# The memory's products behind a tenancy of scores, and the first block's q projected whole before k

## The chip, the cores and the metric

One core of one Trainium2 chip runs the whole kernel. The metric is the device time of one launch in microseconds (us). For every execution the profile also gives its span on the core, some 1.7 us shorter than the time, and the mean granted clock of TensorE, where 1.000 is full speed. Ratios below are the mean time of one kernel's fast runs over that of the other's of the same rounds, so they are not quite the ratio of the medians that stand beside them. All runs here count as fast, those with a mean clock of 0.998 too, and every kernel named below gave correct results.

## The reference, cut to what matters

The kernel is a transformer block over 2048 tokens of width 1024: layer norm, attention of 32 heads in four blocks of 512 tokens with a running memory, a projection, a second layer norm and a gated network of width 3584.

```python
g = sigmoid(beta)
for s in range(4):                       # blocks of 512 tokens
    p = softmax(qs @ ks.T * scale + mask)
    a_dot = p @ vs
    num = phi(qs) @ M                    # what earlier blocks left
    den = phi(qs) @ z + 1e-6
    outs.append(g * (num / den) + (1 - g) * a_dot)
    M = M + phi(ks).T @ vs               # "products for the memory's state"
    z = z + phi(ks).sum(tokens)
h  = x + o @ wo
h2 = h + (silu(ln(h) @ w1) * (ln(h) @ w3)) @ w2
```

## The kernel before

TensorE works in three tilings. Full matmuls use the whole array (128*128 in the views). Scores take four row tiles at once ("tenancies" of the banks that ScalarE's exponentials then empty; the four matmuls of the first start within 0.01 us, at 20.760 to 20.770 in before's trace). The attention's sums take four column tiles (128*32), many small matmuls in one go, and the products for M and z are column tiles too. In the kernel before they are an operation of their own, which the scheduler put into the column stretches:

```python
def memory(self, s, half, gr):
    ...                                  # cut
    def emit(e, gr):
        ...                              # 64 matmuls of 33 columns
        e.matmul(self.ps[32*j:32*j+32, ...], pkn[:, 4*i+kc, 32*j:32*j+32],
                 v[:, kc, g0+i, j, 0:33], start=kc == 0, stop=kc == 3,
                 tile_position=(0, 32*j))
    o = self.g.op("pe", 16 * 42.0, emit, ...)
    o.mode = "col"
    ...                                  # VectorE adds the bank to Macc
```

The first block's tokens come in four tiles x0 to x3. In the head of the kernel q and k are projected for half of their columns, token quarter by token quarter as the tiles get ready, and the other half follows whole:

```python
loads = [x0, x1, wq[:, :, 0:256], x2, x3, wk[:, :, 0:256],
         wq[:, :, 256:512], wk[:, :, 256:512], wv]        # put in words here
work = [(w, i, Group(...)) for w in (wq, wk) for i in range(2)]
for c0 in range(0, 512, 128):
    for w, i, gr in work:                # 8 matmuls of 128 columns
        ...
```

TensorE starts with warm-up matmuls on zeros, `self.warm(12)`, and one more, `self.warm(1, ...)`, between x0's transposes and q's first matmuls.

The softmax here doesn't subtract the row's maximum and nothing guards it: scores larger than these inputs give would overflow.

## Time and profile before

| kernel before | us |
|---|---|
| times of three runs | 895.78, 896.09, 897.34 |
| span of the profiled execution | 895.0 |
| TensorE busy, share of the span | 98% |
| first 128-column matmul of q | 7.70 |
| all 160 matmuls of 128 columns done (128 of projections, 32 transposes) | 18.07 |
| first scores | 20.76 |
| issue hole in the fifth set of products | 1.21 |

TensorE bounds the kernel, so what counts is where it stands or changes tiling. The lines of the views are shown in the prediction. A line of a timeline reads: start in us, busy time, engine, source line, operation, output and inputs by name, tile shape, element shape, count, and in brackets how long the engine was idle before it and what ended that. PE is TensorE and PEld its weight loads, DVE is VectorE, ACT ScalarE, POOL GpSimd and SP SyncE, whose queue issues the transfers (all that the page lists are its).

### The profile page before, as it was taken

Reading aid. Unit: us, or ns where it says so; the run is one execution under the profiler, and the core shown is the slowest. Engines: PE = TensorE matmul, PEld = TensorE weight load, DVE = VectorE, ACT = ScalarE, POOL = GpSimd, SP = SyncE. Lnnn points to the kernel's source line nnn. Section 1 sums busy time; section 2 is a strip of 40 time slices with the busy share of each in tenths; the row PEclk is TensorE's granted clock in tenths of the full one; section 3 lists DMA queues with packets and bytes.
Section 4 is the critical chain, followed back from the end, with each engine's and each line's share of the span. In section 5 each row is a group of like instructions: output and inputs, shape, how many; then the busy total and the mean of one; then the engine's idle time right before and its main releaser. Section 6 shows DMA issues by size and latency. Waiting matters only on the chain.

```text
span 895.0 us, 13604 instructions
## 1 busy us (share of the span) xinstructions
PE 880.6 (98%) x5833; PEld 403.4 (45%) x5921; DVE 417.6 (47%) x631; ACT 287.9 (32%) x306; POOL 173.8 (19%) x226
## 2 busy tenths in 40 slices
PE   8999999999999999999999999999999999999998
PEld 5343444444444444444444444444444444444445
DVE  5784848585848485754555311211334333331111
ACT  6767766656565646111111100000111111110000
POOL 2553445353534343100200000000000000000000
PEclk9999999999999999999999999999999999999999
DMA  7899755634541221753475211113223221301110
GB/s 235 227 212 271 187 142 147 187 92 130 165 99 57 72 70 58 225 153 92 120 224 140 85 36 36 30 46 90 64 60 94 71 71 48 95 24 41 40 37 30
DMA packets 146540, 96.32 MB, mean 108 GB/s; under 512 B 45488, under 2 KB 133680, under 8 KB 146480
## 3 DMA queue, kind: packets, MB, share of 16 engines
q1 hardware_dynamic: 146480, 95.45, 38.8%
q8 instruction: 47, 0.77, 0.4%
q14 instruction: 13, 0.11, 0.0%
HBM read 76.55 MB, written 8.39 MB: 95 GB/s over the span
## 4 chain that ended last, share of the span: by engine, by line
PE 97%; issue 1%; DVE 1%; DMA 1%; ACT 0%; SPq 0%; ACTq 0%; DVEq 0%
PE ps L708 89%; PE ps L1107 4%; PE ps L1057 3%; DMA xs<-in_A_x_dram 1%; PE ps L985 0%; PE ps L1184 0%; ACT et L1069 0%; PE ps L1100 0%; DVE t L1260 0%; DVE hm L1265 0%; PE ps L720 0%; SPq L299 0%; DVE R L1163 0%; ACT sg L1257 0%; DVE Nsb L1171 0%
## 5 line engine op out<-in xcount | busy, mean ns | idle before, releaser
L708 PE MATMUL ps<-hnT,w1b 128*128 128x512 bf16 x876 | 218.4, 379 | 1.4 <-issue 0.3
L708 PE MATMUL ps<-hnT,w3b 128*128 128x512 bf16 x873 | 217.4, 379 | 1.5 <-issue 0.5
L1257 ACT ACTIVATE sg<-ps 128x512 bf16<-128x512 f32 x112 | 66.9, 597 | 403.1 <-PE ps L708 403.1
L708 PE MATMUL ps<-w2b,hm 128*128 128x512 bf16 (+1 forms) x907 | 195.3, 372 | 0.9
L1069 ACT ACTIVATE et<-ps 128x2048 bf16<-128x2048 f32 x80 | 150.0, 1875 | 39.3 <-PE ps L1057 38.9
L1260 DVE SCALAR_TENSOR_TENSOR t<-sg,ps 128x512 bf16<-128x512 bf16 x112 | 76.8, 685 | 169.4 <-ACT sg L1257 169.2
L708 PEld LDWEIGHTS ps<-w2b,hm 128*128 128x128 bf16 x924 | 90.4, 98 | 103.2
L708 PEld LDWEIGHTS ps<-hnT,w1b 128*128 128x128 bf16 x896 | 86.5, 98 | 105.5 <-issue 8.2
L708 PEld LDWEIGHTS ps<-hnT,w3b 128*128 128x128 bf16 x896 | 86.5, 98 | 105.4 <-issue 2.9
L1078 POOL TENSOR_SCALAR_AFFINE_SELECT et<-et 128x512 bf16<-128x512 bf16 x96 | 84.0, 881 | 126.2 <-ACT et L1069 126.0
L1265 DVE SCALAR_TENSOR_TENSOR hm<-t,ps 128x512 bf16<-128x512 bf16 x112 | 76.7, 686 | 50.5 <-PE ps L708 47.9
L1289 DVE TENSOR_TENSOR ob<-hr,ps 128x512 bf16<-128x512 bf16 (+1 forms) x33 | 22.1, 671 | 143.0 <-PE ps L708 143.0
L708 PE MATMUL ps<-wo,oT 128*128 128x512 bf16 x249 | 60.7, 380 | 0.6 <-issue 0.3
L708 PE MATMUL ps<-xnT,wp 128*128 128x512 bf16 (+1 forms) x345 | 59.7, 320 | 1.4 <-issue 0.6
L708 PE MATMUL ps<-hnT,wp 128*128 128x512 bf16 x250 | 59.0, 380 | 0.7 <-issue 0.6
L708 PEld LDWEIGHTS ps<-xnT,wp 128*128 128x128 bf16 x352 | 27.7, 98 | 26.9 <-issue 3.6
L708 PEld LDWEIGHTS ps<-wo,oT 128*128 128x128 bf16 x256 | 23.9, 98 | 29.8 <-issue 2.9
L708 PEld LDWEIGHTS ps<-hnT,wp 128*128 128x128 bf16 x256 | 23.6, 98 | 29.8 <-issue 3.8
L1200 POOL TENSOR_TENSOR oT<-Nsb,R 128x512 bf16<-128x512 f32 x23 | 35.8, 1569 | 4.1 <-DVE R L1197 4.1
L1163 DVE STREAM_TRANSPOSE R<-Rc 128x1024 f32<-128x1024 f32 x28 | 33.6, 1222 | 0.1
L1229 DVE TENSOR_TENSOR h<-h,ps 128x512 bf16<-128x512 bf16 x32 | 21.7, 680 | 25.1 <-PE ps L708 24.9
L1057 PE MATMUL ps<-qT,kT 32*128 32x128 bf16 (+3 forms) x512 | 31.7, 301 | 0.0
(82 smaller groups left out, 520.9 us busy)
## 6 DMA issues: line engine op xcount, KB each, us to landing
w1b<-in_B_w_dram SPq DMA_DIRECT2D x28, 512.0 KB, 3.9
w3b<-in_B_w_dram SPq DMA_DIRECT2D x28, 512.0 KB, 3.8
wp<-in_A_wv_dram SPq DMA_DIRECT2D x8, 1024.0 KB, 5.5
wp<-in_A_wq_dram SPq DMA_DIRECT2D x7, 1024.0 KB, 5.9
wp<-in_A_wk_dram SPq DMA_DIRECT2D x7, 1024.0 KB, 5.7
w2b<-in_B_w_dram SPq DMA_DIRECT2D x7, 1024.0 KB, 8.0
xs<-in_A_x_dram SPq DMA_DIRECT2D x16, 256.0 KB, 5.6
h<-in_A_x_dram SPq DMA_DIRECT2D x16, 256.0 KB, 3.7
```

The source lines that it names most:

```text
L708: return [e.matmul(p[0](gr), p[1], p[2], start=p[3], stop=p[4]) for p in part]
L1057: ins.append(e.matmul(self.bank(gr, j, 512 - 128 * kc, off), k[r, g0 + g, 128 * kc:128 * kc + 128], q[r, g0 + g, 128 * kc:512], start=True ...
L1069: return [e.activation(et[:, :, :], src, AF.Exp, scale=self.scale)]
L1078: self.pool_op(lambda e, v=v, pat=pat: e.affine_select(v, v, pattern=pat, compare_op=ALU.is_ge, fill=0.0, base=0, channel_multiplier=-1), ...
L1107: ins.append(e.matmul(self.ps[32 * i:32 * i + 32, b * 512 + 128 * kc:(b + 1) * 512], lhsT(i, kc, j), at[i, kc][:, j, :], start=kc == 0 and ...
L1163: return self.dve_op(lambda e: e.transpose(out, src), dve_ns(1024), [Rc[:, t, 2 * n:2 * n + 2, :]], [dst], 2)
L1200: self.either(lambda e, out=out, Ns=Ns, R1=R1: e.tensor_tensor(out, Ns, R1, op=ALU.add), 512, 2, [Ns, R1], [out], 2)
L1229: self.g.op("dve", dve_ns(512), lambda e, gr, hs=hs: [e.tensor_tensor(hs, hs, self.bank(gr), op=ALU.add)], reads=[hs], writes=[hs], cls=1, ...
L1257: self.g.op("act", act_ns(512), lambda e, gr, sg=sg: [e.activation(sg, self.bank(gr), AF.Tanh, scale=0.5)], writes=[sg], cls=0, group=gg)
L1260: e.scalar_tensor_tensor(t1, sg, 1.0, self.bank(gr), op0=ALU.add, op1=ALU.mult)], reads=[sg], writes=[t1], cls=0,
L1265: e.scalar_tensor_tensor(dst, t1, 0.5, self.bank(gr), op0=ALU.mult, op1=ALU.mult)], reads=[t1], writes=[dst], cls=0,
L1289: self.g.op("dve", dve_ns(n), lambda e, gr, hs=hs, ob=ob, n=n: [e.tensor_tensor(ob, hs, self.bank(gr, 0, n), op=ALU.add)], reads=[hs], wri ...
```

## The change

Its intent: the products share an excursion with a tenancy of scores, so that the stretches of small column matmuls get shorter, and the weights of the first block are read in rows of 1 KB, with q of all four groups of columns projected while the tokens arrive and k whole behind it. All matmuls stay. The core of the diff (the table of some 470 schedule shifts was searched anew and is left out):

```diff
-        loads.insert(2, (wq[:, :, 0:256], sq[:, :, 0:256]))
-        loads.insert(5, (wk[:, :, 0:256], sk[:, :, 0:256]))
-        loads += [(wq[:, :, 256:512], sq[:, :, 256:512]), (wk[:, :, 256:512], sk[:, :, 256:512]),
-                  (wv[:, :, :], sv)]
+        loads = [x[0] + (1.0,), x[1] + (0.68,), x[2] + (0.9,), (wq[:, 0:4, :], sq[:, 0:4, :], 0.85),
+                 (wq[:, 4:8, :], sq[:, 4:8, :], 0.8), x[3] + (0.68,), (wk[:, :, :], sk, 0.8),
+                 (wv[:, :, :], sv, 0.8)]
...
-        var, mean, op = self.ln_act(t, x) if t % 2 else self.ln_stats(
-            t, x, 1, (self.applied[0],) if t else ())
+        var, mean, op = self.ln_act(t, x) if t == 1 else self.ln_stats(t, x, 1)
...
-        work = [(w, i, Group([(5,), (6,), (7,), (4,)], safe=True))
-                for w in (wq, wk) for i in range(2)]
+        work = [Group([(5,), (6,), (7,), (4,)]) for _ in range(4)]
...
+        for i in range(4):
+            self.project(0, "k", 0, i, wk)
...
-            self.scores(s, g0, i, parts, at)
+            self.scores(s, g0, i, parts, at, i == MEM and s < 3)
...
+            if state:
+                ins += add(e, mem.banks[0])      # the 64 products, after the scores
```

## The prediction

The sum is 896.09 - 0.95 + 0.6 - 0.5 + 0.1 = 895.3 us. Its pace of TensorE is that of before's trace: from start to start 56 ns for 128 columns (24 from 10.92 to 12.27) and 216 ns for 512 (behind 21.09). The split of the 0.43 us of an excursion into 0.21 and 0.22, or 0.11 for a change, is the estimate from those 216 ns. The landings of q's halves "at about 7 and 9" are an estimate too, from the 319 GB/s of a window of before.

> **What bounds the kernel now.** I read the page's busy table and chain first, then the timeline of the TensorE by start times, then the timeline of all engines over the first 20 us, last the one-microsecond windows of the DMA. The page first:
>
> ```profile
> span 895.0 us, 13604 instructions
> PE 880.6 (98%) x5833; PEld 403.4 (45%) x5921; DVE 417.6 (47%) x631; ACT 287.9 (32%) x306; POOL 173.8 (19%) x226
> PE   8999999999999999999999999999999999999998
> PE 97%; issue 1%; DVE 1%; DMA 1%; ACT 0%; SPq 0%; ACTq 0%; DVEq 0%
> ```
>
> The chain that ended last is TensorE for 97%, no other engine is over half busy, and the clock row of the page is at 9 tenths or more throughout. So nothing matters but matmuls, the mode changes between them, and places where TensorE stands. Next the timeline of PE (start, duration, group); only the starts are used, as durations of pipelined matmuls overlap.
>
> ```profile
> 20.76 0.40 PE L1057 MATMUL ps<-qT,kT 32*128 32x512 bf16 x4
> 21.09 2.76 PE L708 MATMUL ps<-xnT,wp 128*128 128x512 bf16 x12
> 23.78 0.40 PE L1057 MATMUL ps<-qT,kT 32*128 32x128 bf16 x8
> ...
> 54.59 0.72 PE L1107 MATMUL ps<-et,v 128*32 128x512 bf16 x16
> 55.14 0.69 PE L985 MATMUL ps<-v,pkn 128*32 128x33 bf16 x64
> 55.66 1.28 PE L1107 MATMUL ps<-et,v 128*32 128x512 bf16 x32
> ...
> 269.22 0.51 PE L985 MATMUL ps<-v,pkn 128*32 128x33 bf16 x42
> 270.81 0.32 PE L985 MATMUL ps<-v,pkn 128*32 128x33 bf16 x22 [1.07 <-issue]
> 270.95 0.73 PE L1107 MATMUL ps<-et,v 128*32 128x512 bf16 x16
> ```
>
> From one tenancy of scores to the next (20.76 to 23.78) are 3.02 us: 12 full matmuls of 512 columns at 0.216 us make 2.59, so an excursion into scores costs 0.43 us. About 0.21 of it is streaming (four tiles at once, 512 columns), 0.22 is the two mode changes. The 64 small products for the memory's state (line 985) take 0.52 us between two groups of the column mode they share, with no change paid at all. Summing the whole stretch from 15 to 361 us in this way, every tenancy agrees within 0.02 us but one: the fifth set of products took 1.73 us (269.22 to 270.95) in place of 0.52, and the 1.21 us above are an "issue" wait: TensorE waited for nothing the profile shows. That is the only hole there.
>
> The head is different:
>
> ```profile
> 6.45 0.63 PE L720 MATMUL ps<-ident,xs 128*128 128x128 bf16 x8 [0.88 <-DVE xs L862]
> 7.70 1.07 PE L708 MATMUL ps<-xnT,wp 128*128 128x128 bf16 x16 [0.41 <-DMA wp<-in_A_wq_dram]
> 8.34 1.29 DVE L831 BATCH_NORM_STATS2 lnst<-xs 128x6 f32<-128x512 bf16 x2 [1.05 <-DMA xs<-in_A_x_dram]
> 9.06 1.06 ACT L817 ACTIVATE oT<-xs 128x1024 bf16<-128x1024 bf16 x1 [1.35 <-DMA xs<-in_A_x_dram]
> 10.92 1.51 PE L708 MATMUL ps<-xnT,wp 128*128 128x128 bf16 x24 [0.20 <-DVE lnve L857]
> 14.95 5.88 PE L708 MATMUL ps<-xnT,wp 128*128 128x128 bf16 x67
> ```
>
> Before 14.95 TensorE did 72 projection matmuls of 128 columns and 32 transposes, 104 x 56 ns = 5.8 us of useful work; the other 9.1 us are warm-up matmuls and waiting for tokens and weights. From 14.95 on it never stands: 56 more of 128 columns (3.1 us) end at 18.07, 12 of 512 columns end before the first scores at 20.76. The DMA in that head (columns: busy of each engine, clock, DMA share, GB/s):
>
> ```profile
> 6.00:7.00 1.00, 0.55 (x9) 0.52 (x9) 0.76 (x3) 0.80 (x2) 0.12 (x1) 1.00 1.03 361
> 10.00:11.00 1.00, 0.80 (x10) 0.53 (x11) 0.87 (x4) 0.75 (x5) 0.00 (x1) 1.00 1.06 279
> 13.00:14.00 1.00, 1.00 (x22) 1.00 (x19) 0.86 (x3) 0.29 (x1) 0.44 (x1) 1.00 1.05 319
> ```
>
> Token rows of 2 KB move at about 361 GB/s, weight rows of 512 B (the quarter-width q and k) at about 279, rows of 1 KB (v) at about 319, the DMA full each time.
>
> [...]
>
> **The change part by part.** The multiset of matmuls is the same: in the order of both programs I counted 3665 full ones of 512 columns, 160 of 128, 80 score tenancies, 8 column stretches, 6 retrievals, 6 sets of products. So no work goes.
>
> *Products after scores.* They leave the column stretch, where they cost 0.52 us and no change, and stand between a tenancy of scores and full matmuls. Sequence row to full becomes row, column, full: one more change each, about 0.10 us, 6 x 0.10 = +0.6 us. The streaming stays 6 x 0.52. In return the stretch of small instructions is broken: before, up to 196 matmuls with their weight loads came in one go, 392 instructions in about 5 us, and in one of six the issue gave out for 1.21 us. After, at most 132 matmuls stand together, and 72 around the products. I expect the hole to go, but it may be a matter of luck that other executions do not share (three timed runs spread by 1.56 us), so I credit 0.5 of 1.21.
>
> *The head, replayed with the durations of before.* Loads are now x0, x1, x2, q's weights in two halves of the contraction, x3, then k and v whole. x0 and x1 land at about 3.5 and 4.1 as before, x2 0.7 later at 4.8 (was 8.3), the q halves at 0.52 MB / 319 = 1.65 us each, at about 7 and 9[...], x3 near 9.8 (was 9.0), k near 13. The VectorE now puts half of x2's statistics (0.65) ahead of x0's variance op, so x0's normalized half comes at 7.2 rather than 6.3 and q's first 16 matmuls at 8.2 rather than 7.7. From there TensorE is fed: x1 and x2 normalized between 8.4 and 10.2, and 16 + 4 + 8 + 52 matmuls of q plus 24 transposes run to about 13.7. x3's statistics start near 10.2, its chain (two statistics 1.3, a copy 0.4, aggregate and variance 0.35, power 0.6, two applications 0.8) reaches the transposes at 13.5 to 13.9, just in time. Then 8 transposes and 48 of q: 56 x 56 ns = 3.1, to 16.8; a wait for a bank's evacuation, about 0.3, and k starts at full width near 17.1. That point has the same 160 matmuls of 128 columns behind it as 18.07 had before. Gain -0.95 us. Everything after it is TensorE at the same rate.
>
> *Extra risk of earlier products.* They now need the transposed keys and all of v some 10 us earlier. For the first half I place them near 45 us, the second transpose's landing near 39, so no wait; I allow +0.1 for one of the six.
>
> Sum: 896.09 - 0.95 + 0.6 - 0.5 + 0.1 = 895.3 us.
>
> **Rivals.** (1) The waits of the head only move: x0's chain is held behind x2's statistics and x3 lands later, so k starts at 18 or later. For it: x3 gives up 0.8 us at the DMA, its statistics move to VectorE, which then carries three tiles. Against it: TensorE has 112 q matmuls to do meanwhile. It would give about 896.3. (2) The change from row to column tiles is dear, or products wait for transposed keys: 0.3 us each or one wait of 2 us, about 897. The first transpose took 5.2 us from issue to landing in the busy stretch near 55 us; against it is the slack above. (3) The issue hole belonged to every execution and goes in all, and row to column is nearly free: about 894.0. (4) The evacuation load moves and ScalarE's exponentials set the pace; against it stand 32% busy and a tenancy every 3.02 us for an exponential of 1.88.
>
> **Range and chances.** The parts are 0.5 to 1.2 us each, and can add to between -2.3 and +0.8, so 893.8 to 896.7 holds 8 in 10; most likely 895.3. A change of 2% would be 18 us. All that TensorE waits, the head included, is about 10 us, so faster by 2% is all but excluded (0.005), and slower would need a wait in each of the stretches, which a schedule with no work added does not suggest (0.005). Within 2%: 0.99.
>
> **What would show it.** Head: k's first full-width matmul near 17.1, the first scores near 21.5 (20 full matmuls precede them in the order, not 12, so later than 20.76 is no loss), no wait over 0.5 us on TensorE after 8.2. Products: about 0.62 us each, from their start to the start of the full matmuls after them, and the column stretches shorter by 0.52. No issue hole over 0.5 us between 20 and 360 us. The prediction is wrong if k starts after 18, if the products show a wait on a DMA transpose, or if issue holes appear elsewhere in like amount.

## The result, and the profile after

The kernel after took 898.75 us in the median of six runs (897.44 to 899.95), the kernel before of the same rounds 896.54 (895.78 to 897.72): ratio 1.0022, with a 95% interval of 1.0009 to 1.0035. Under a threshold of 2% that is "the same", but the time lies 2 us above the upper end of the predicted range. Of the six executions three had a mean clock of 1.000 (spans 895.7, 896.9, 895.8) and three of 0.998 (897.1, 898.2, 897.8). The profile is of the fastest, so it can show only part of the loss. The page, answering to the lines of before:

```profile
span 895.7 us, 13605 instructions
PE 881.1 (98%) x5830; PEld 403.0 (45%) x5921; DVE 415.2 (46%) x626; ACT 287.8 (32%) x307; POOL 175.8 (20%) x227
PE 96%; issue 1%; DMA 1%; SPq 1%; ACT 1%; DVE 0%; ACTq 0%
```

TensorE still bounds it; new in the chain are SyncE's queue and ScalarE with 1% each. The timeline of TensorE's head, and below it ScalarE's:

```profile
7.37 0.63 PE L719 MATMUL ps<-ident,xs 128*128 128x128 bf16 x8 [0.83 <-DVE xs L866]
8.53 1.05 PE L707 MATMUL ps<-xnT,wp 128*128 128x128 bf16 x16 [0.31 <-DMA wp<-in_A_wq_dram]
14.86 2.62 PE L707 MATMUL ps<-xnT,wp 128*128 128x128 bf16 x44
18.63 4.26 PE L707 MATMUL ps<-xnT,wp 128*128 128x512 bf16 x19 [1.15 <-ACT qT L730]
22.82 0.40 PE L1064 MATMUL ps<-qT,kT 32*128 32x512 bf16 x4
```

```profile
16.75 0.90 ACT L682 ACTIVATE gcol<-beta 32x8 f32<-32x8 bf16 x4 [1.54 <-DMA beta<-in_A_beta_dram]
17.67 1.57 ACT L730 ACTIVATE qT<-ps 128x512 bf16<-128x512 f32 x3
```

q's first 16 matmuls start at 8.53, q ends near 17.3, and then TensorE stands: k needs a bank that ScalarE's copy of q has to free, and that copy stands in ScalarE's order behind the four tanh of beta, whose load came only just ahead of 16.75. The record of k's first matmul is missing (19 of 20 are there), so k starts one matmul earlier than its line, at 18.63 - 0.22 = 18.41. In before the same point was 18.07.

Of the steady state, the first set of products and the end of the last column stretch:

```profile
46.15 0.40 PE L1064 MATMUL ps<-qT,kT 32*128 32x128 bf16 x8
46.48 0.66 PE L985 MATMUL ps<-v,pkn 128*32 128x33 bf16 x64
...
380.07 2.02 PE L1119 MATMUL ps<-et,ones 128*32 128x512 bf16 x52
382.47 0.51 PE L1119 MATMUL ps<-et,ones 128*32 128x384 bf16 x12 [0.39 <-issue]
```

The hole of before in the fifth set of products is gone. In its place are two in the column stretches, 0.57 us ending at 382.47 and another of 0.45 us ending at 336.05 (each measured as the stretch's length over that of the undisturbed ones).

The profiled execution adds up so: k starts 0.34 later, the six sets of products cost 0.46 more (measured below), the holes are 1.02 in place of 1.21. That is +0.61, and the spans differ by +0.7. The median differs by +2.2, so some 1.5 us come from things that this trace does not hold.

### The profile page after: what moved, and what is told of

Read it like the earlier page. It is cut to its first block, busy times and chain, and to the rows that moved or that the text cites. A ratio compares the mean times of both kernels' runs of the same rounds, so it can differ in the third digit from the quotient of the medians.

```text
span 895.7 us, 13605 instructions
## 1 busy us (share of the span) xinstructions
PE 881.1 (98%) x5830; PEld 403.0 (45%) x5921; DVE 415.2 (46%) x626; ACT 287.8 (32%) x307; POOL 175.8 (20%) x227
## 4 chain that ended last, share of the span: by engine, by line
PE 96%; issue 1%; DMA 1%; SPq 1%; ACT 1%; DVE 0%; ACTq 0%
PE ps L707 88%; PE ps L1119 4%; PE ps L1064 3%; DMA beta<-in_A_beta_dram 1%; SPq L298 1%; PE ps L985 0%; PE ps L1194 0%; DVE t L1270 0%; ACT et L1082 0%; ACT sg L1267 0%; PE ps L1112 0%; DVE hm L1275 0%; ACT gcol L682 0%; ACT qT L730 0%; DVE ob L1299 0%
```

## The experiments

Fourteen kernels ran in four batches; the kernel before ran beside each. A change of the head alone was meant to be one of them, but its schedule did not come out without a new search of the shifts, so the parts are taken apart by moving single operations in the finished orders. Each kernel left one kept trace, so what is read in a trace holds for one of its executions.

### The two kernels again

No edit. A second look, for the spread and for whether the holes recur.

> The kernel before, unchanged, for more executions with their clocks. If the 2.2 us between the two kernels come from a TensorE clock that falls for one window in some executions of the kernel after (three of its six showed 0.998, which over 897 us is some 1.8 us more), this kernel's executions should show 1.000 nearly always. If 0.998 is as frequent here, the clock does not explain the difference. The hole of 1.2 us inside the fifth set of products near 269 us: if it belongs to the program's order it is there again, within 0.3 us; if it is chance it is gone or elsewhere.

> The kernel after, unchanged, for more executions and a second trace. Clock theory: 0.998 in about half of the executions, and those are 1.5 to 2 us longer than the ones at 1.000. The holes in the column stretches near 336 us (0.45) and 382 us (0.57) are there again if they belong to the order of instructions. The late start of k's matmuls (18.4) and ScalarE's wait for beta to 16.7 are there again in any case.

Before: 896.95 us, ratio 1.0002 (0.9989 to 1.0016), all five executions at a clock of 1.000, and the hole again in the fifth set of products, 1.20 us. After: 898.69 us, ratio 1.0023 (1.0010 to 1.0036); one execution at 1.000, four at 0.998. Its trace has the two holes of after and a third of 1.2 us that ends at 67.28. So the place of a hole belongs to a kernel's instruction order, not to chance, though its size varies and the third opened in only one of the two traces. The lower clock is a habit of after: of the 38 executions of the kernel before that ran beside these batches one showed it. I had expected the executions at 0.998 to be 1.5 to 2 us longer than those at 1.000. Here their spans were 896.4 to 899.4 against 896.6 for the one at 1.000, which is the one with the third hole; how much the lower clock costs is taken up below.

### beta ahead of k's weights

```diff
+        sp.remove(b); b.start = wk.start - 1e-3     # the load of beta,
+        sp.insert(sp.index(wk), b)                  # issued before that of wk
```

> The kernel after with one transfer moved: the load of beta is issued ahead of k's weights in place of behind v's. Theory that ScalarE's four tanh of beta, which stand in its order before the copy of q's first bank and wait for beta's landing at 16.7, hold k's first matmul: k starts near 17.5 in place of 18.4 and the time falls by 0.9 to 1.1 us. Rival, that the copy of the bank waits for q's last matmuls anyway: k starts at 18.2 or later, within 0.2 us the same time.

It took 898.31 us, ratio 1.0015 (1.0002 to 1.0028), again four of five executions at 0.998. ScalarE and TensorE in its trace:

```profile
15.42 0.88 ACT L682 ACTIVATE gcol<-beta 32x8 f32<-32x8 bf16 x4
16.71 1.71 ACT L730 ACTIVATE qT<-ps 128x512 bf16<-128x512 f32 x3 [0.41 <-PE ps L707]
```

```profile
15.17 6.94 PE L707 MATMUL ps<-xnT,wp 128*128 128x128 bf16 x63
22.04 0.40 PE L1066 MATMUL ps<-qT,kT 32*128 32x512 bf16 x4
```

The tanh are over before q ends, the copy waits for TensorE and not for beta, and q and k run in one group of 63 recorded matmuls with no wait between them. The first scores come at 22.04, 0.78 before after's, although q began later here. So the wait ahead of k was the late beta, worth 0.8 us. The span of the profiled execution is 0.8 below that of after's (894.9 against 895.7, both at 1.000), but the median fell by only 0.4 us against the second look at after, where I had expected 0.9 to 1.1: this was not the whole of the loss.

### Other warm-up, other places in the stream

```diff
-        self.warm(12)
+        self.warm(6)                                # matmuls of 512 columns
+        ...                                         # 64 of 32 columns
```

Six long warm-up matmuls give way to 64 short ones, which moves each later TensorE instruction by 116 places (58 matmuls, each with its weight load).

> The kernel after with half of its twelve warm-up matmuls replaced by 64 small ones, so that the rest of TensorE's instructions stand 116 places further on. Theory[...]: the holes near 336 and 382 us go, or move, or change by more than 0.3 us, and others may come up; total within 1.5 us. Rival, that the holes come from the work around these stretches (transfers, waits): they stay where they are with the same length.

What the run tests is whether the holes follow the place in the stream.

It took 898.24 us, ratio 1.0012 (1.0000 to 1.0025). All holes in the column stretches are gone, but the gain did not come: four of five executions had 0.998, the profiled one too, and for once the trace shows where. In the windows of one microsecond the five engine columns are TensorE's matmuls, its weight loads, VectorE, ScalarE and GpSimd; then come TensorE's granted clock, the DMA's share and its GB/s:

```profile
7.00:8.00 1.00, 0.00 (x0) 0.00 (x0) 0.97 (x4) 0.06 (x1) 0.59 (x2) 1.00 1.03 333
10.00:11.00 1.00, 1.00 (x13) 1.00 (x11) 0.93 (x4) 0.00 (x0) 0.04 (x1) 0.50 1.08 384
11.00:12.00 1.00, 1.00 (x12) 1.00 (x11) 0.74 (x2) 0.00 (x0) 0.00 (x0) 0.50 1.11 357
```

TensorE stood from 5.8 to 8.60, and the clock records of the trace then read 0.5 for 3.41 us, from 9.61 to 13.02: the windows give 0.80 for 9 to 10, 0.50 for each of the three to 13, and 0.99 for 13 to 14. At the half clock four transposes took 0.43 us (11.41 to 11.84), after it 0.22 (13.53 to 13.75). So 3.41 us of full work lose, by estimate, 1.7 us, and 1.7 over 895 is the missing 0.002 of the mean clock. The drop came 1.0 us after TensorE had begun again; what sets that moment is not shown. I had not looked for a drop, because the profile of before showed none at all (its mean clock is 1.000).

Here the transposes of x0 were late because x2's statistics stand ahead of x0's variance op in VectorE's order, and x2 landed only at 6.55. The clock is not all that ate the gain: the trace also has a wait of 1.0 us for a late token tile at 186.80, and the span of the one execution at 1.000 (896.6) lies among those of the four at 0.998 (895.5 to 897.2).

### Is the clock's drop the head's idle time?

Three kernels ask it. In `x0_first` x0's chain goes ahead of x2's statistics on VectorE, in `warm_long` TensorE is kept busy longer, and in `before_late_x0` the head of the kernel before gets a like gap.

```diff
# x0_first: order of VectorE only
+        put_before(self.first[0], self.stats2)   # x0's variance op
+        lst[i:j + 1] = self.first[1:] + late     # x0's two applications, then x2's statistics
# warm_long
-        self.warm(12)
+        self.warm(15, like=12)
-                self.warm(1, [self.g.ops[-1]])
+                self.warm(3, [self.g.ops[-1]], 1)
# before_late_x0: two idle statistics, 1.3 us, ahead of x0's variance op
+            held = [self.dve_op(... e.bn_stats(a, x[:, 0:512]) ...),
+                    self.dve_op(... e.bn_stats(b, x[:, 512:1024]) ...)]
```

> Kernel after with only the VectorE order of the head changed: x0's variance op and both of its normalizing applications come ahead of x2's statistics (TensorE's order is the same). Theory of the clock (executions of after in which TensorE stands long enough between warm-up and x0's transposes lose half their clock for one window of 3.41 us): transposes of x0 start near 6.5 as in before, no wait on x2's landing before them, at most one of five executions with a mean clock under 1.0, and the time falls by 1 to 1.7 us against after, to about 897.2. Rival (the clock drop belongs to the longer rows of the weight loads or to chance, the head's end is set by ScalarE's tanh of beta): q's start moves but k starts at 18.0 to 18.6 as in after, most executions keep 0.998, ratio 1.0015 to 1.0025.

> Kernel after with 15 warm-up matmuls in place of 12 and 3 in place of 1 between x0's transposes and q's first matmuls; nothing else moves in order, 116-fold padding is not used. Theory of the clock: [...]all five executions show a mean clock of 1.000 and the time falls by about 1.2 us on the median against after, to about 897.4; k's start is 18.0 to 18.5 as in after's undisturbed executions. Rival (the clock drop follows something other than TensorE's idle time[...]): 0.998 in three or more of five, ratio 1.002 or above, since five extra warm-up matmuls can only add.

> Kernel before with two idle statistics (1.3 us together) on VectorE ahead of x0's variance op, so that x0's transposes start near 7.7 instead of 6.45; its matmuls keep their order. Theory of the clock: TensorE idles over a microsecond more after the warm-up, and the half clock window of 3.41 us comes up in at least two of five executions of a kernel that had it in none of fourteen; those are 1.7 us longer, the others +0 to +1.2 us; ratio 1.001 to 1.003. Rival (the drop belongs to after's loads of 1 KB rows or to its many first q matmuls): all five at 1.000, and the time rises by 0.3 to 1.2 us only.

| kernel | us | ratio, 95% | clocks of the executions |
|---|---|---|---|
| x0_first | 898.97 | 1.0025 (1.0011 to 1.0040) | five at 1.000 |
| warm_long | 898.26 | 1.0017 (1.0004 to 1.0030) | five at 1.000 |
| before_late_x0 | 897.76 | 1.0016 (1.0002 to 1.0030) | two at 1.000, three at 0.998 |

All three agree on the clock: two ways of shortening or breaking up TensorE's idle time ended the drops (in the trace of x0_first it is 0.63 us and, after the transposes, 1.25), and idle time put into before brought them on (1.70 us, ahead of the transposes at 7.92, in its trace). The spans of before_late_x0 were 895.4 and 895.4 at 1.000 and 897.6, 896.0 and 897.6 at 0.998. Its windows:

```profile
6.00:7.00 1.00, 0.22 (x2) 0.00 (x0) 0.64 (x2) 0.97 (x2) 0.24 (x1) 1.00 0.92 304
11.00:12.00 1.00, 0.91 (x9) 0.64 (x8) 0.91 (x3) 0.72 (x2) 0.00 (x0) 0.50 1.15 290
```

But the times of the two mended kernels missed what I expected. In x0_first the transposes came at 6.44 as in before, and yet nothing followed from it:

```profile
6.44 0.63 PE L719 MATMUL ps<-ident,xs 128*128 128x128 bf16 x8 [0.63 <-DVE xs L870]
8.54 1.07 PE L707 MATMUL ps<-xnT,wp 128*128 128x128 bf16 x16 [1.25 <-DMA wp<-in_A_wq_dram]
67.77 0.35 PE L1125 MATMUL ps<-et,v 128*32 128x256 bf16 x8 [1.07 <-issue]
```

q's first matmuls waited for the weights, which had only hidden behind x0's chain, and began at 8.54, as in after; k, still behind the late beta, began at 18.45 (the line's 18.67 less the one matmul missing), as the rival had it. This execution, the longest of the five, also has the hole that ends at 67.77, a wait of 1.1 us for a late token tile and one of 0.7 for a late weight of the gated network. Both are transfers that landed late in that one trace; why is not settled here. Of warm_long only the fastest execution was traced (span 895.1), so what kept its median 0.9 us above what I expected is not shown.

### Where the holes come from

`before_pad` moves the kernel before by the same 116 places, `before_shift` (a batch later) by 64:

```diff
-        self.warm(12)
+        self.warm(6)      # before_pad, then 64 of 32 columns
+        self.warm(9)      # before_shift, then 35 of 32 columns
```

> Kernel before with half of its 12 warm-up matmuls replaced by 64 small ones of 32 columns, which moves every later TensorE instruction by 116 places in its stream and nothing else. Theory (the issue hole of 1.2 us belongs to where the small matmuls fall in the instruction stream): the hole in the fifth set of products near 269 vanishes and the time falls by 1.2 us, ratio 0.9987, unless another stretch of small matmuls is hit, which the trace would show as an issue wait of 0.4 to 1.2 us. Rival (the hole belongs to the 196 small instructions in one go, wherever they fall): it stays at 269, ratio 1.000.

> Kernel before with 9 long and 35 small warm-up matmuls in place of 12 long ones: the later TensorE stream is moved by 64 places. Theory of place: the hole of 1.2 us near 269 changes its size or goes, and others may appear elsewhere; the time changes by between -1.2 and +5 us in step with the sum of holes that the trace shows, all else equal. Rival (the two holes of 2.5 us under the shift of 116 came from something else, such as the small warm-up matmuls themselves): two holes of 2.5 us near 58 and 99 again.

They took 901.22 us (ratio 1.0058, 1.0037 to 1.0079) and 902.68 us (1.0068, 1.0056 to 1.0081). In both the hole near 269 is gone as expected, and two far larger ones are there. Those of before_pad:

```profile
58.50 0.78 PE L1112 MATMUL ps<-et,v 128*32 128x128 bf16 x20 [2.54 <-issue]
99.55 1.27 PE L1112 MATMUL ps<-et,v 128*32 128x512 bf16 x31 [2.35 <-issue]
```

After the second of before_pad the clock records read 0.5 for 3.41 us from 101.0: the seven full matmuls recorded from 100.97 took 3.09 us, where the seven behind the first hole, from 59.45, took 1.60. In before_shift the mean clock of the profiled execution was 0.998 as well. So a hole can cost its length and, by the estimate above, 1.7 us on top (one of six executions of before_pad, at a mean clock of 0.992, took 906.46). Half of my expectation for before_pad, "the time falls by 1.2 us", was wrong; its proviso came true. In before_shift the two holes come again near 59 and 100, which is what its rival, that the small warm-up matmuls bring them on, expected. Two kernels speak against that rival: after_pad and mended_pad (below) have 64 and 58 such matmuls and no hole in any column stretch.

With this the holes can be placed. I counted each TensorE instruction of the built programs (a matmul as two, with its weight load; a semaphore step as one); the weight loads and semaphore steps that the traces record ahead of a hole give the same places. The number of the first one after each hole:

| kernel | hole ends at, us | place in the stream | modulo 256 |
|---|---|---|---|
| before, twice | 270.8, 270.5 | 5313 | 193 |
| before_pad | 58.50, 99.55 | 1217, 1985 | 193 |
| before_shift | 59.21, 100.10 | 1217, 1985 | 193 |
| after, after_again, mended | 335 to 337, 382 to 383 | 6337, 7105 | 193 |
| after_again | 67.28 | 1218 | 194 |

Every hole stands at one place modulo 256, give or take one. The page's list of queues has something of that count: its instruction queue brought 0.77 MB in 47 packets, of 16 KB each. From the first of them (17.14) to the last (885.94) before's trace holds 11335 matmuls and weight loads, 246 to a packet, with semaphore steps and missing records not among them. And each of these holes ends 2.2 to 2.8 us after such a packet starts. From this I infer that a packet brings 256 of TensorE's instructions and that a hole is TensorE waiting for it; no record of the trace says so itself. A block, below, is the 256 instructions from one such place to the next. In a stretch of small column matmuls a block is soon used up: in 3.41 us ahead of the hole of before, in 2.72 and 2.74 ahead of those of before_pad, in 5.64 and 5.86 ahead of those of after, in 6.50 and 6.88 ahead of those of mended (below). In the first five of these the packet started 2.4 to 4.2 us after the block began, in mended 4.7 and 5.4, and the sum closes: in before 2.42 to the packet, 2.25 from there to the end of the hole, less the block's 3.41, is the gap of 1.26. On this account a block that lasts longer than both together shows no hole, and one that doesn't leaves a hole of the difference. A short block alone does not make a hole: before used up the block that ends at 136.51 in 3.8 us and before_pad the one that ends at 230.21 in 2.7, with no hole of note, and their packets had started 1.2 and 0.4 us after the block began. The block ahead of after_again's third hole lasts 5.9 us in after too, with the same instructions; in after its packet started 0.3 us before the block began and no hole came, in after_again 4.5 us after. What sets the delay of the packet stays open, so this account places the holes but does not foretell which of them open.

### Both mends of the head, and the offset

`mended` is after with beta early and the longer warm-up. The others add short warm-up matmuls in place of long ones so that the later stream stands 116, 64 or 240 places further than in after:

```diff
-        self.warm(15, like=12)
+        self.warm(10)     # mended_pad, then 58 of 32 columns
+        self.warm(13)     # mended_64, then 29
+        self.warm(5)      # mended_240, then 125
```

The last two test the account of blocks: from after's issue times I reckoned for every offset in how many microseconds each block would be used up. At 64 none lasts under 6.6 us, at 240, the worst, four last 4.1 to 4.7.

> Kernel after with both mends of its head: beta's load issued ahead of k's weights, and 15 and 3 warm-up matmuls in place of 12 and 1. Theory (after loses 0.8 us of its head to ScalarE's tanh of a late beta, and 1.7 us to a half clock window in most executions): all five at a clock of 1.000, k's first full-width matmul near 17.4, median about 1.2 to 2 us under after's, that is 896.8, ratio 0.9998 to 1.001. Rival (what makes the executions of after spread lies in the steady state: late loads of h and w3b, issue holes; the head is worth nothing in the end): ratio 1.0015 to 1.002 as the single mends showed.

> As mended, but 10 long and 58 small warm-up matmuls in place of 15 long ones, so that the later TensorE stream is moved by 116 places as in the run that had no issue holes. Theory of place: no hole over 0.3 us in any stretch of small matmuls, and the time falls by 1 to 1.5 us below mended, to about 895.5, ratio 0.9985 to 0.9995. Rival (the holes are worth nothing because other waits take their place): same as mended within 0.5 us.

> Kernel after with the mended head and its later TensorE stream moved by 64 places against after. Reckoned from after's own issue times: at this offset no block of 256 TensorE instructions would be used up in under 6.6 us. Theory of blocks (all the holes found so far stand at one place modulo 256 in the stream, and come where the block before was used up in under about 6 us): no hole over 0.3 us between 50 and 400 us, as in mended_pad, and the time within 0.6 us of mended_pad's 895.9, where kernel before at the same offset of 64 had 902.7. Rival (mended_pad's gain was this one offset's luck or came from its longer warm-up): holes of 0.5 us and more, time 897 to 898 as mended.

> As mended_64 but moved by 240 places, the worst offset that the same reckoning finds for after's order: four blocks used up in 4.1 to 4.7 us. Theory of blocks: holes of 0.5 to 2 us at up to four places, all at place 193 to 194 modulo 256 of the stream, 3 to 6 us in all, and the time 2 to 5 us above mended_64 (898 to 901)[...]. Rival (offset matters little for after's order): within 1 us of mended_64.

| kernel | us | before beside it | ratio, 95% | holes in its trace, us |
|---|---|---|---|---|
| mended | 897.89 | 896.84 | 1.0012 (0.9999 to 1.0025) | 0.64 and 1.23 |
| mended_pad | 895.87 | 896.84 | 0.9988 (0.9975 to 1.0002) | none |
| mended_64 | 896.89 | 897.23 | 0.9997 (0.9985 to 1.0010) | none |
| mended_240 | 899.40 | 897.23 | 1.0023 (1.0009 to 1.0036) | 1.4 and 0.4 |

The first three had all executions at 1.000; mended_240, whose shorter warm-up left TensorE idle again, had two of five at 0.998. The head of mended_pad, and what its TensorE waited for once its warm-up had begun (total in us, times, longest):

```profile
15.16 6.94 PE L707 MATMUL ps<-xnT,wp 128*128 128x128 bf16 x63
22.03 0.39 PE L1071 MATMUL ps<-qT,kT 32*128 32x512 bf16 x4
```

```profile
PE ps L707 <- issue: 4.6, 29, 0.2
PE ps L719 <- DVE xs L871: 0.7, 1, 0.7
PE ps L707 <- DVE t L1277: 0.2, 1, 0.2
```

The 29 issue waits of 0.2 us each have the length of one matmul of 512 columns; after's trace has them too, and that of mended_64, in which no record is missing, has none. So they are read as missing records. No other issue wait is left, and none for k. From mended to mended_pad the median fell by 2.0 us, and the holes of mended's trace sum to 1.9, though mended_pad's first scores come 0.36 later (22.03 against 21.67); some 0.5 us of the fall has no account here. So mended_pad is where after would have been without its three faults: 895.87 us, some 0.1% under before, with an interval that just includes 1. mended_64, with k's start 0.4 us later than in mended_pad, is even with before. Of what I expected, mended's clock and head came true and its time missed by 1.1 us; mended_64 had no hole, as the account of blocks asks, but lay 1.0 us above mended_pad and not within 0.6. Mended itself shows that 6.6 us is no safe length, as its blocks of 6.50 and 6.88 us left holes.

The offset matters to both orders, but not equally. Moved by 64 places, the order of before costs 902.68 us and that of after 896.89; moved by 116, 901.22 and 898.24 (after_pad) or, mended, 895.87. The warm-ups differ between these, and with them the clock, so the offset is not all of each difference. Of the three offsets tried for it, the kernel before stands at the one that suits it best. mended_240 held the place (its larger hole is at 1473, again 193 modulo 256) but not the amount: two of four reckoned holes came, 1.8 us in place of 3 to 6. The spans of its executions at 0.998 (897.3 and 897.7) lie among those at 1.000 (895.9 to 898.1), so how its 2.5 us over mended_64 divide is not shown.

### What the products cost in their new place

```diff
+                ins += add(e, mem.banks[0], (0, 1))   # half of them ahead of the scores
...
-                ins += add(e, mem.banks[0])
+                ins += add(e, mem.banks[0], (2, 3))   # half behind
```

> Kernel after with each set of products cut in two, half ahead of the scores and half behind them: full, column, row, column, full in place of full, row, column, full, so one more mode change in each of six excursions and nothing else. Theory of the mode cost: each of the six takes about 0.1 us longer, 0.6 us in all, seen as the time from the first full matmul before to the first after. Rival (a change between column and row tiles is nearly free, and after's slower products have another cause): under 0.03 us each. The trace decides; the total time cannot show 0.6 us well.

It took 899.26 us (1.0029, 1.0012 to 1.0045; four runs), which tells little. The trace does, after's first set again being the one near 46 us above:

```profile
45.93 0.38 PE L985 MATMUL ps<-v,pkn 128*32 128x33 bf16 x32
46.24 0.40 PE L1065 MATMUL ps<-qT,kT 32*128 32x128 bf16 x8
46.56 0.38 PE L985 MATMUL ps<-v,pkn 128*32 128x33 bf16 x32
```

From the last full matmul ahead of the excursion to the first recorded behind it are 1.461 us in five of six sets of after and 1.483 here. One more change of tiling cost 0.02 us, not 0.10; the rival was right on this. The price of the new place itself is read best in mended_64, in whose trace no record is missing:

```profile
46.39 0.66 PE L992 MATMUL ps<-v,pkn 128*32 128x33 bf16 x64
46.98 1.69 PE L707 MATMUL ps<-xnT,wp 128*128 128x512 bf16 x7
```

The set takes 0.60 us from its start to the full matmul's, where it took 0.52 in a column stretch of before: 6 x 0.077 = 0.46 us in all. The trace of products_split also shows a drop of the clock after a hole: 2.0 us ending at 68.38, then 0.5 of the clock for 3.41 us from 69.39 (its windows of 2 us from 68 on give 0.85, 0.50 and 0.80).

## Why the prediction was wrong

*Products after scores, +0.6.* Right in size: +0.46. Its reason, a flat 0.10 us for each change, was wrong, since an added change cost 0.02.

*The issue hole, -0.5.* This step failed. I took the hole of before for something that long stretches bring on, or luck, and gave half of it as a gain. It belongs to a place in the stream where two blocks of 256 instructions, as counted above, meet. The changed order left that place and met two others, sometimes three: 1.02 us in its own profile, over 2 in that of after_again. The shorter stretches do make an order less sensitive, as the offsets of 64 and 116 show, but after's own offset is not a good one.

*The head, -0.95.* This step failed too; it came out at +0.34. The three terms: q's weights landed at 8.44 and not "near 7", so q began 0.33 late (in the second trace of after they landed at 6.86 and q, held by x0's chain, began at 8.65, so the two limits lie close together); q then took some 0.2 longer than I reckoned; and the evacuation wait of "about 0.3" was 1.1, because I had not asked what stands ahead of that copy in ScalarE's order. The beta that I left out of the list of loads was the one that arrived last. With beta early the wait is gone and k starts at about 17.6 (22.04 less 20 matmuls and one change), which is 0.8 of the 1.3 us by which k's start missed.

*Waits for transposed keys, +0.1.* None showed in any trace.

*What the sum did not contain.* The clock. Three of six executions of after, and four of five in the second round, show the mean of 0.998 that one half-clock window of 1.7 us gives; five kernels with a shorter or broken-up idle time in the head never did, in 25 executions. That in the unprofiled executions of after the window lies in the head is inferred from this, not seen. What it cost is less sure: in six runs with executions at both clocks the mean span at 0.998 was longer by 1.0 to 2.2 us (after 1.6), but in after_pad and mended_240 by -0.3 and 0.2. With 0.34 + 0.46 - 0.19 = 0.61 for the profiled execution, about 1.7 in half to four fifths of the executions and a third hole in some, the median of +2.2 is reached in size, though the last two terms can't be weighed exactly. The upper end of the range was also drawn too low: the parts' own +0.8 would give 896.9, not 896.7, and no part stood for the clock.

Of the rivals, the first came nearest in mechanism: the waits of the head only moved, and k started after 18. None reached the time. Two of the three signs that I named as proof against me, k after 18 and holes elsewhere in like amount, are what the trace shows.

## What to carry to other kernels

Before crediting a gain in a head, follow each evacuation in its engine's own order: here four tanh of 0.90 us in all, on data that landed at 16.7, held k back by 0.8 us. Where dense small instructions wait for "issue", count their places. All the holes placed here stand at 193 or 194 modulo 256; for after's mended order an offset of 64 or 116 left none and one of 240 left 1.8 us, and before's order took 896.5, 901.2 and 902.7 us at three offsets, so two kernels should not be compared at one offset each. A gap of two microseconds or so on TensorE may be charged twice, as itself and as a window at half clock: those of 2.0 us in products_split, 2.35 in before_pad and 2.8 in after_pad were, though one of 2.54 in before_pad was not. So look at the mean clock of every execution, not only at the profiled one.

## What the runs show of the hardware

- Instructions: holes of 0.4 to 3.4 us at places 193 or 194 modulo 256, with blocks used up in 2.7 to 6.9 us and 2.2 to 2.8 us from the packet's start to the hole's end. How far ahead of TensorE the packets run was not measured.
- Clock: 1.7 us without a matmul in the head of before_late_x0, and holes of 2.0 us in products_split and 2.35 in before_pad, were followed by a window at half clock, of 3.41 us in the last two. Not every one was: a first hole of 2.54 us in before_pad was not (the seven full matmuls behind it took 1.60 us), nor 1.71 us in the head of products_split (16 matmuls of 128 columns took 0.90 us after it, 8.48 to 9.38). What decides is not shown.
- Changes of tiling: 0.22 us for the two changes of a scores excursion (the estimate above), and, measured, 0.08 for products behind scores and 0.02 for one more change between column and row tiles.
- DMA: windows of one microsecond in the head moved 345 to 388 GB/s in after (9 to 17 us), mostly weight rows of 1 KB, and 256 to 289 in before (9 to 13 us) while weight rows of 512 B moved; some windows mix these with other transfers.
